# Adding transfers that no longer wait for transposing ones, in a convolution and feed-forward kernel

## The chip, the cores and the metric

One core of one Trainium2 chip. The metric is the device time of one execution in microseconds (us), as a median over runs.

## The reference, cut to what matters

Per head and token, seven weights are made by a softmax; they weigh the token and the six before it (a causal convolution whose weights depend on the position). A layer norm and a two-layer feed-forward block with a residual follow.

```python
batch, seq, d_model = (8, 4224, 192)      # 8 heads of 24 channels, 7 taps, 4 * 192 hidden channels
def _attn_ref(x, weight_gen):
    w = np.exp(weight_gen - np.max(weight_gen, axis=-1, keepdims=True))
    w = w / (np.sum(w, axis=-1, keepdims=True) + 1e-09)
    ...
    out = np.einsum('bshk,bskhg->bshg', w, x_unf)
def _moe_ref(x, g_ln, w_ch1, w_ch2):
    xn = (x - mu) / np.sqrt(var + 1e-06) * g_ln
    ch = np.maximum(xn @ w_ch1, 0.0) @ w_ch2
    return (x + ch).astype(np.float32)
```

## The kernel before, in words

**Tiling.** The 33,792 tokens lie on 128 partitions, 264 on each. They pass through in chunks of 4 tokens a partition (67 chunks; the first two have 2), the norm works on parts of 4 or 8, and the feed-forward block on 66 groups of 4, that is 512 tokens.

**Stages.** SP loads x and the softmax's input. The softmax (L466 to L499) runs on VectorE, GpSimd and ScalarE. For a chunk, VectorE multiplies x by the weights, two taps at a time, into buffers `pr` and, for one tap, into `y` (L544). The seven results are then summed. Adding transfers do part of it: GpSimd issues a DMA that adds one half of a `pr` buffer to its other half (`dma_add`, L550; two for each chunk from the fifth on, 126 in all). GpSimd itself adds four buffers to `y` (L547, 252 times); a `pr` buffer is free for VectorE's next product when GpSimd has read it. There are seven `pr` buffers. ScalarE takes sums and squares for the norm (L597, L602), normalises into `xh` (L657) and copies it to fp16, the upper part of `hl` (L677); GpSimd subtracts for the lower part (L690). Then a transposing transfer, issued by SP, turns `hl` into `xT` (L694, one for each group, 66 in all). There are two `hl` buffers and three `xT` buffers.

**Feed-forward block.** TensorE makes the hidden layer of a group in three units of 36 products each (L712) into two PSUM buffers `ph` in turn. ScalarE (relu, L727) and VectorE (the rest, L729) evict a unit; when VectorE's eviction ends, the buffer is free for the next unit but one. The output of an earlier group follows in two halves of 72 matmuls (L763) between the units; the second half waits for a nop on SP (L773) behind the first. VectorE adds the residual (L815), SP stores (L823).

**Order.** Every operation has a place in one list, written out by hand (`PLACE`, L32 to L226). `Plan.order` (L272) sorts by it, picks buffers, and so fixes the order on every engine and queue; engines take their instructions in that order and wait by semaphores. The same function keeps two kinds of transfer apart. An operation may have a kind: "add" for the adding transfers (L576), "turn" for the transposing ones (L694, through `sp`). `last` holds the latest operation of each of these two kinds, and `o.behind` is the latest one of the other kind (L287, L288). After all operations have been issued, L1016 and L1017 make an instruction wait until the transfer in `o.behind` has landed. So an adding transfer, issued by GpSimd, waits for the last transpose ahead of it in the list, and a transpose, issued by SP, for the last adding transfer. What stands behind a waiting instruction in the same engine's order waits too.

Of the kernel before, what the change touches and what calls it, by code (L numbers as in the profile page):

```python
# [238 lines left out]
class Plan:  # L239
# [32 lines left out]
    def order(self):  # L272
        out = sorted(self.ops, key=lambda o: o.place)
        tenant = {p: [None] * len(t) for p, t in self.pools.items()}
        done, last = set(), {"add": None, "turn": None}

        def freed(t):
            return -1 if t is None else max(x.place for x in t.ops)

        for o in out:  # L280
            assert o.deps <= done, "an operation is placed ahead of what it needs"
            for b in o.bufs:
                if b.slot is None:
                    b.slot = min(range(len(tenant[b.pool])), key=lambda i: freed(tenant[b.pool][i]))
                    assert freed(tenant[b.pool][b.slot]) < o.place, "no buffer is free"
                    tenant[b.pool][b.slot] = b
            if o.kind in last:  # L287
                o.behind, last[o.kind] = last["turn" if o.kind == "add" else "add"], o  # L288
            done.add(o)
        return out  # L290

# [756 lines left out]
```

## Time and profile before

| | |
|---|---|
| Time, median of 3 runs | 856.57 us (855.5 to 859.03) |
| Profiled execution: its time, its span | 856.96 us, 855.2 us |
| TensorE (PE) busy | 823.4 us, 96% |
| VectorE (DVE) busy | 763.0 us, 89% |
| GpSimd (POOL) busy | 728.7 us, 85% |
| ScalarE (ACT) busy | 646.1 us, 76% |
| Transposing transfers, adding transfers | 66, 126 |
| Mean granted TensorE clock | 0.992 |

All times inside the execution count from the start of the span. An instruction's row gives its start, its duration, its engine, line and operation, what it writes and reads, how many equal ones are merged, and in brackets how long the engine had been idle before it and what ended that. "DMA xT<-hl" is the landing of a transposing transfer, "DMA pr<-pr" that of an adding one. A duration of a matmul includes its passage through the pipeline, so matmuls overlap, and their pitch is shorter than their duration.

### The profile page before, as it was taken

The numbers are of one execution on the slowest core, as the hardware profiler recorded it, in microseconds if no ns is written. First come the engines' busy times: TensorE is split into PE (matmuls) and PEld (weight loads), VectorE is DVE, ScalarE is ACT, GpSimd is POOL, SyncE is SP. The second block draws the span as 40 slices with busy tenths as digits, with TensorE's granted clock in tenths as the row PEclk, the third lists the DMA queues.
The fourth block names the chain that finished last, engine by engine and source line by source line (L and its number), as shares of the span: only waits on it lengthen the run. The fifth ranks groups of instructions, "written<-read, shape, count | busy, mean of one in ns | idle before, by whom it ended". The sixth has DMA issues, their size and how long they took to land. (4 is left out here: it accounts for less than half of the span.)

```text
span 855.2 us, 37740 instructions
## 1 busy us (share of the span) xinstructions
PE 823.4 (96%) x16691; PEld 803.7 (94%) x16691; DVE 763.0 (89%) x863; ACT 646.1 (76%) x1797; POOL 728.7 (85%) x489
## 2 busy tenths in 40 slices
PE   4959999999999999999999999999999899999997
PEld 4548999999999999999999999999999899999997
DVE  7999999999999999999999999999999899673442
ACT  3888898787778888778869887878878678667521
POOL 7999999999899999999999889999986878964100
PEclk9979999999999999999999999999999999999999
DMA  9878878898878898788988799798876675845123
GB/s 219 192 176 171 166 153 186 162 199 192 188 169 198 192 190 162 181 164 189 203 187 203 163 184 197 165 168 198 190 152 151 159 137 134 158 80 108 37 74 94
DMA packets 146411, 140.91 MB, mean 165 GB/s; under 512 B 108487, under 2 KB 110415, under 8 KB 146247
## 3 DMA queue, kind: packets, MB, share of 16 engines
q1 hardware_dynamic: 127799, 88.95, 44.3%
q0 software_dynamic: 18144, 49.55, 31.3%
q8 instruction: 130, 2.13, 1.1%
q14 instruction: 34, 0.28, 0.1%
q10 hardware_dynamic: 304, 0.00, 0.0%
HBM read 36.43 MB, written 25.95 MB: 73 GB/s over the span
## 5 line engine op out<-in xcount | busy, mean ns | idle before, releaser
L547 POOL TENSOR_TENSOR y<-y,pr 128x768 f32<-128x768 f32 x252 | 514.2, 2206 | 15.4 <-DMA pr<-pr 6.1
L712 PE MATMUL ph<-xT,c_w 64*128 64x256 f16 x7128 | 417.0, 271 | 8.4 <-DVE hlo L729 8.0
L712 PEld LDWEIGHTS <-c_w 64*128 64x128 f16 x7128 | 383.8, 95 | 17.0 <-issue 11.1
L763 PE MATMUL po<-c_w2h,hh 64*128 64x192 f16 x3120 | 387.8, 243 | 0.8 <-SPq L773 0.4
L763 PE MATMUL po<-c_w2h,hlo 64*128 64x192 f16 x3120 | 387.8, 243 | 0.0
L763 PE MATMUL po<-c_w2l,hh 64*128 64x192 f16 x3120 | 387.7, 243 | 0.0
L544 DVE TENSOR_TENSOR pr<-x,wn 128x1536 f32<-128x1536 f32 (+1 forms) x193 | 332.1, 1738 | 5.5 <-POOL y L547 3.9
L763 PEld LDWEIGHTS <-hh 64*128 64x128 f16 x6240 | 307.2, 94 | 2.1 <-SPq L773 1.0
L729 DVE SCALAR_TENSOR_TENSOR hlo<-ph,hh 128x1024 f16<-128x1024 f32 x198 | 239.5, 1217 | 55.8 <-ACT hh L727 55.7
L727 ACT ACTIVATE hh<-ph 128x1024 f16<-128x1024 f32 x198 | 199.4, 1013 | 117.3 <-PE ph L712 114.8
L763 PEld LDWEIGHTS <-hlo 64*128 64x128 f16 x3120 | 175.3, 94 | 0.0
L690 POOL TENSOR_TENSOR hl<-xh,hl 128x768 f16<-128x768 f32 x66 | 132.8, 2031 | 33.3 <-ACT hl L677 33.2
L550 POOL DMA_DIRECT2D pr<-pr x126 | 130.1, 1233 | 27.4 <-DMA xT<-hl 14.4
L657 ACT ACTIVATE xh<-y,s 128x192 f32<-128x192 f32 x264 | 125.1, 535 | 22.1 <-DVE s L641 11.9
L602 ACT ACTIVATE junk<-y,s 128x192 f32<-128x192 f32 x264 | 116.1, 443 | 0.0
L597 ACT ACTIVATE junk<-y 128x192 f32<-128x192 f32 x264 | 92.2, 351 | 27.9 <-POOL y L547 27.5
L815 DVE SCALAR_TENSOR_TENSOR y<-po,c_fs,y 128x768 f32<-128x768 f32 (+1 forms) x66 | 65.7, 997 | 3.3 <-PE po L763 3.3
L544 DVE TENSOR_TENSOR y<-x,wn 128x768 f32<-128x768 f32 (+1 forms) x67 | 62.1, 933 | 0.2
L677 ACT ACTIVATE hl<-xh 128x768 f16<-128x768 f32 x66 | 55.0, 837 | 4.2 <-DMA xT<-hl 3.3
L602 ACT ACTIVATION_READ_ACCUMULATOR junk<-y,s 128x1 f32 x264 | 50.0, 189 | 0.0
L597 ACT ACTIVATION_READ_ACCUMULATOR junk<-y 128x1 f32 x264 | 49.8, 189 | 0.0
L469 POOL TENSOR_TENSOR e<-w,mx 128x672 f32<-128x672 f32 (+2 forms) x23 | 39.4, 1713 | 2.8 <-DVE mx L467 2.7
(75 smaller groups left out, 315.3 us busy)
## 6 DMA issues: line engine op xcount, KB each, us to landing
pr<-pr POOLq DMA_DIRECT2D x126, 384.0 KB, 6.2
x<-in_x_dram SPq DMA_DIRECT2D x65, 384.0 KB, 5.5
out_dram<-y SPq DMA_DIRECT2D x64, 384.0 KB, 4.4
w<-in_weight_gen_dram SPq DMA_DIRECT2D x21, 336.0 KB, 5.0
pr<-in_moe_w_ch_dram SPq DMA_DIRECT2D x2, 576.0 KB, 5.1
xT<-hl SPq DMA_TRANSPOSE x66, 3.6
hh<-in_moe_w_ch_dram SPq DMA_DIRECT2D x1, 768.0 KB, 10.1
out_dram<-y SPq DMA_DIRECT2D x4, 192.0 KB, 3.2
```

Of the source, the lines that this page charges most:

```text
L544: E.tensor_tensor(out=ov, in0=xv, in1=wv, op=ALU.mult)
L547: Q.tensor_tensor(out=flat(0), in0=flat(0), in1=flat(k), op=ALU.add)
L550: return Q.dma_start(flat(to), flat(k), accum_op=ALU.add, max_dma_last_dim=CHUNK * D * 4)
L597: A.activation(junk[t % 2], at(y)[:, j, :], AF.Identity, scale=-1.0 / D, accum_out=at(s4)[:, 3, t : t + 1])
L602: A.activation(junk[2 + t % 2], at(y)[:, j, :], AF.Square, bias=at(s4)[:, 3, t : t + 1], accum_out=at(s4)[:, 0, t : t + 1])
L657: A.activation(paired(xh, t), at(y)[:, i, :].rearrange("p (c q) -> p c q", q=P // 2), AF.Identity, bias=at(s4)[:, 3, g + t : g + t + 1], s ...
L690: lambda xh=xh, hl=hl: Q.tensor_tensor(out=halves(hl, True), in0=pairs(xh), in1=halves(hl, False), op=ALU.subtract),
L712: T_.matmul(ph[:, r, v * 2 * P : (v + 1) * 2 * P], W["w1"][rows, WB[r][c], w, f : f + P], xv[rows, a, c, :, :], start=(v == 0 and k == 0), ...
L727: lambda: A.activation(at(hh)[:, us, :], at(ph), AF.Relu), [ph], [(hh, u)])
L729: lambda: V.scalar_tensor_tensor(out=at(hlo)[:, us, :], in0=at(ph), scalar=0.0, in1=at(hh)[:, us, :], op0=ALU.max, op1=ALU.subtract),
L763: made.append(T_.matmul(at(po)[:, z, e * D : (e + 1) * D], token(b, 2 * z + e, j)[rows], W[w][rows, j, :], start=(ph == 0 and e == 0 and k ...
L815: V.scalar_tensor_tensor(out=ysl, in0=at(po)[:, zs[0] : zs[-1] + 1, : 2 * D], scalar=W["fs"][:, 0:1], in1=ysl, op0=ALU.mult, op1=ALU.add)
```

## The change

An adding transfer gets no `o.behind` any more, so L1017 makes no wait for it. A transposing transfer still gets the last adding one. Order, buffers and all other waits come from the same list as before.

```diff
             if o.kind in last:
-                o.behind, last[o.kind] = last["turn" if o.kind == "add" else "add"], o
+                o.behind, last[o.kind] = last["add"] if o.kind == "turn" else None, o
             done.add(o)
```

## Rows read from the trace of the kernel before

**Rows 1.** The page's part 1: engine, busy us (share of the span), instructions.
```profile
PE 823.4 (96%) x16691; PEld 803.7 (94%) x16691; DVE 763.0 (89%) x863; ACT 646.1 (76%) x1797; POOL 728.7 (85%) x489
```
**Rows 2.** Waits of PE: who waited for whom, us in total, times, longest.
```profile
PE ph L712 <- DVE hlo L729: 8.0, 9, 2.3
```
**Rows 3.** Timeline of PE around its two late gaps: start us, us, what.
```profile
668.53 0.26 PE L763 MATMUL po<-c_w2l,hh 64*128 64x192 f16 x2
668.61 0.26 PE L763 MATMUL po<-c_w2h,hlo 64*128 64x192 f16 x2
...
671.13 3.56 PE L712 MATMUL ph<-xT,c_w 64*128 64x256 f16 x36 [2.26 <-DVE hlo L729]
...
677.73 0.51 PE L712 MATMUL ph<-xT,c_w 64*128 64x256 f16 x6
...
748.66 0.26 PE L763 MATMUL po<-c_w2h,hlo 64*128 64x192 f16 x2
749.95 0.40 PE L712 MATMUL ph<-xT,c_w 64*128 64x256 f16 x4 [1.03 <-DVE hlo L729]
```
**Rows 4.** Stretches: length, busy us (instructions) of PE, PEld, DVE, ACT, POOL, clock, DMA share, GB/s.
```profile
671.10:672.00 0.90, 0.87 (x14) 0.84 (x15) 0.86 (x2) 0.67 (x1) 0.90 (x2) 0.81 0.98 321
672.00:673.00 1.00, 1.00 (x14) 0.85 (x11) 1.00 (x2) 0.17 (x1) 1.00 (x2) 0.50 1.09 215
```
**Rows 5.** The chain of work that ended last, in order of time: start us, us, what.
```profile
646.01 7.56 DMA pr<-pr
...
653.70 4.11 DMA xT<-hl
...
684.81 1.97 PE ph L712 x36
686.77 2.97 PE po L763 x72
```
**Rows 6.** Timeline of DVE, 600 to 673 us and at 748 us.
```profile
640.09 3.41 DVE L544 TENSOR_TENSOR pr<-x,wn 128x1536 f32<-128x1536 f32 x2
...
660.45 0.17 DVE L630 TENSOR_SCALAR wn<-s 128x8 f32<-128x8 f32 x1 [1.75 <-ACT junk L602]
660.53 1.22 DVE L729 SCALAR_TENSOR_TENSOR hlo<-ph,hh 128x1024 f16<-128x1024 f32 x1
...
668.19 1.75 DVE L544 TENSOR_TENSOR pr<-x,wn 128x1536 f32<-128x1536 f32 x1 [2.17 <-POOL y L547]
...
748.67 1.23 DVE L729 SCALAR_TENSOR_TENSOR hlo<-ph,hh 128x1024 f16<-128x1024 f32 x1 [3.99 <-ACT hh L727]
```
**Rows 7.** Timeline of ACT, the waits ahead of the two gaps.
```profile
657.83 0.84 ACT L677 ACTIVATE hl<-xh 128x768 f16<-128x768 f32 x1 [1.42 <-DMA xT<-hl]
...
745.36 0.36 ACT L597 ACTIVATE junk<-y 128x192 f32<-128x192 f32 x1 [3.29 <-POOL y L547]
```
**Rows 8.** Waits of POOL: who waited for whom, us in total, times, longest.
```profile
POOL pr L550 <- DMA xT<-hl: 14.4, 9, 4.9
```
**Rows 9.** Timeline of POOL: its long waits for a transpose, and the subtraction at 661.06.
```profile
504.51 2.66 POOL L550 DMA_DIRECT2D pr<-pr  x3 [2.45 <-DMA xT<-hl]
...
625.98 1.77 POOL L550 DMA_DIRECT2D pr<-pr  x2 [1.80 <-DMA xT<-hl]
...
643.10 1.77 POOL L550 DMA_DIRECT2D pr<-pr  x2 [1.53 <-DMA xT<-hl]
...
658.09 0.87 POOL L550 DMA_DIRECT2D pr<-pr  x1 [4.91 <-DMA xT<-hl]
...
661.06 2.25 POOL L690 TENSOR_TENSOR hl<-xh,hl 128x768 f16<-128x768 f32 x1
...
725.99 3.57 POOL L550 DMA_DIRECT2D pr<-pr  x4 [1.68 <-DMA xT<-hl]
```
**Rows 10.** Timeline of PE, the product that uses the transpose of 653.70.
```profile
661.80 4.11 PE L712 MATMUL ph<-xT,c_w 64*128 64x256 f16 x72
```
**Rows 11.** Issue to landing of all transfers of a line: L694 transposing, then L550 adding.
```profile
DMA to landing us min/median/max: 3.2/3.6/6.5
...
DMA to landing us min/median/max: 3.8/6.2/10.7
```

## The prediction

> **What bounds the kernel now.** I read the page first. TensorE is busy for 823.4 us of a span of 855.2 [rows 1], so only time in which TensorE stands still, or runs slowly, can be won. The table of waits narrows this: from the first product to the last, the products waited 8.0 us in nine pieces for VectorE's eviction, which frees the PSUM buffer that the next product writes [rows 2]. The timeline of TensorE places them. Four pieces lie before 70 us, while the pipeline fills, and three are small. Two large ones lie late [rows 3]. At 668.61 the last output matmul starts; its neighbours follow 0.08 us apart, so the next was due at 668.69, and it starts at 671.13: 2.44 us. At 748.66 the same: due 748.74, started 749.95: 1.21 us.
>
> The first of the two costs more than its gap. Behind it the granted clock falls to 0.81 and then to 0.50 [rows 4], half speed. So 36 products and 72 output matmuls, which elsewhere take 1.97 and 2.97 us (4.94 together; the chain of work has both [rows 5]), run from 671.13 to 677.73, 6.60 us [rows 3]: 1.66 us lost to the clock. Behind the gap of 1.21 us no such stretch follows. The two places cost 2.44 + 1.66 + 1.21 = 5.31 us.
>
> Next question: who made VectorE late? In its timeline [rows 6] the late eviction stands behind a product that started at 668.19, after an idle 2.17 us that a GpSimd sum ended (sums free the buffers that products write). Before that VectorE had idled 1.75 us for ScalarE. The eviction of 748.67 waited for ScalarE, and ScalarE's timeline shows why: it stood idle 3.29 us until GpSimd's sum at 745.36 [rows 7]. Both roots are GpSimd being late. GpSimd's own waits name the cause: 14.4 us in nine pieces were spent ahead of an adding transfer until a transposing one had landed [rows 8]. These are just the waits that the change takes away.
>
> **The change, part by part.** It adds no instruction and moves none; 126 adding transfers lose one wait each. Most lose nothing real: by the time GpSimd reached them, the transpose had landed. Only the nine pieces are time, and GpSimd's timeline shows the large ones [rows 9]: 2.45 us at 504.51, 1.80 at 625.98, 1.53 at 643.10, 4.91 at 658.09 and 1.68 at 725.99 (some half a microsecond of two or three of them is the issue itself).
>
> The wait at 504.51 is worth nothing: neither large gap of TensorE lies within 160 us behind it, so products already waiting in buffers hide it. If that cover is gone it is 2.45 us at most.
>
> The first gap. Ahead of it GpSimd loses 1.80 + 1.53 + 4.91 = 8.24 us. Not all of this comes back, because the transposes still wait for adding transfers. Follow the chain of work [rows 5]: the adding transfer of 646.01 takes 7.56 us, and right behind its landing the transpose is sent at 653.70, taking 4.11 us. That transfer was held by the first two waits (3.3 us), but it also needs VectorE's products that end at 640.09 + 3.41 = 643.50 [rows 6]; it can be sent some 2.4 us sooner. So can the transpose, and ScalarE's copy, which idled 1.42 us until that transpose landed [rows 7], and the subtraction that GpSimd starts at 661.06 behind the copy [rows 9]; with the queue of GpSimd empty earlier, that one gains between 2.4 and 4.9 us. The product on VectorE needs 2.17 us. Its idle 2.17 us goes, most of the earlier 1.75 us with it: VectorE is up to 2.17 + 1.75 = 3.9 us earlier there. TensorE then has no gap, keeps its clock, and is 2.44 + 1.66 = 4.10 us earlier. VectorE is 0.2 us short of that, and I give 0.2 us back.
>
> The second gap. GpSimd must be 4.1 + 1.2 = 5.3 us earlier at 745.36 than now. It brings some 3.9 us from before and gains the 1.68 us at 725.99: 5.6 us. This is close, but enough. None of the nine pieces lies behind 750 us: from there TensorE runs through to its end, so what is won reaches the end of the run.
>
> What is late next: VectorE, whose evictions end just ahead of TensorE's need in this stretch. One ends at 660.53 + 1.22 = 661.75 [rows 6], and the product that needs its buffer starts at 661.80 [rows 10]. The issue queue of SP has no more to do; the nops by which the output matmuls change banks stand behind transposes in it as before.
>
> The operation that this trace doesn't have is an adding transfer sent while a transpose is in flight: now neither starts before the other has landed. I bound it from the two groups of landings [rows 11]. A transpose takes 3.2 us at best and up to 6.5 us, and it does meet plain loads and stores; an adding transfer takes 3.8 to 10.7 us. The lower end is no slowing: 3.2 us. The upper is one after the other: 3.2 + 10.7 = 13.9 us. I take 6.5 us at most, since plain transfers on the same queues are nearest to it. The transpose of 653.70 is needed by the product of 661.80 [rows 5, 10], 8.1 us later, so 6.5 us costs nothing, and it would itself be sent 2.4 us sooner.
>
> **The sum.** The profiled execution took 856.96 us (span 855.2 us and 1.8 us around it), 0.4 us over the median of 856.57. 5.31 - 0.2 = 5.1 us less gives 851.9 us for that execution and 851.5 us against the median. A measurement of this kernel can tell about 0.5%, 4.3 us, from no change: faster means below 852.3 us.
>
> **The rivals.**
> *Only the first gap goes.* The four adding transfers of 725.99 are sent sooner but land no sooner, since they now run beside a transpose; GpSimd's sums then wait for the landing instead. The 1.21 us stay: 856.57 - 4.10 = 852.5 us. For it speaks how close the second account was; against it, that these transfers have 3.8 to 10.7 us to land in [rows 11] and the late sum comes 19 us behind them. The Trainium skill, on the page "DMA: Bandwidth & Descriptors", section "Issuing engines are not separate DMA queues", says that transfers started by different engines run on the same 16 DMA engines and interleave, so starting them side by side saves little beyond the issue; by this rule the time is that of this rival, 852.5 us. The trace agrees so far as transposes stretch from 3.2 to 6.5 us.
>
> *VectorE becomes the bound.* GpSimd runs ahead, but the evictions keep TensorE back right after 671 us, and a gap of some 2 us opens there in small pieces. Half of the 2.44 us stays in this way, the clock's 1.66 us are won, and the second gap stays: 1.22 + 1.66 = 2.9 us less, 853.7 us. For it: the margin of 0.05 us just shown. Against it: VectorE's own idle time ahead of the gap was caused by GpSimd.
>
> *The change removes nothing.* ScalarE's copy and the subtraction behind it still wait for a transpose through the buffers, and take the place of the wait: 856.6 us. Against it: the copy's own waits were 1.42 us where GpSimd's was 4.91.
>
> *Slower.* Adding transfers and a transpose in flight hinder each other much more than plain ones. The place is the transpose of 653.70; it decides from 8.1 us on. At 13.9 us it lands at 667.6, TensorE stands for 5.8 us at 661.80, pays the slow clock again (1.7 us), and the old gaps stay because adding transfers land late too: 856.57 + 5.8 + 1.7 = 864.1 us. Nothing here shows that pair, which is why it keeps a chance.
>
> *More.* The small pieces of TensorE's 8.0 us go by the shift as well, with the 0.2 us that I gave back and a wait or two of the output matmuls: about 1.3 us, an estimate, 850.2 us.
>
> **How the numbers follow.** Forecast 0.45, only the first gap 0.17, VectorE 0.14, nothing 0.08, more 0.08, slower 0.08. Of the forecast, about 0.38 lies below 852.3 us; of the first rival 0.07, and all of "more": 0.53 faster. Slower has its rival's 0.08. The other 0.39 is within 0.5%. The range goes from 849.9 us (the better case and the spread of the runs) to 856.9 us (no change); it leaves out the slower rival and the outer parts of two others.
>
> **What would show it.** Right: no wait of an adding transfer for a transpose in GpSimd's table; no gap of TensorE over 1 us after 70 us; a granted clock of 1.00 from 600 to 700 us; TensorE's last product about 5 us earlier. Wrong: the 0.50 stretch still there, or a new wait of GpSimd's sums for the adding transfers, or transposes that take over 8 us. If the products wait for xT itself, the slower rival holds; if they wait for the eviction at other places, VectorE's.

## The result and the profile after

The changed kernel takes 849.37 us, the median of 4 runs (849.22 to 849.53); the kernel before took 857.56 us beside it (4 runs, 855.50 to 859.03). The ratio is 0.9906 [0.9883, 0.9930]. A second set, run later, gave 849.37 us again (5 runs, 849.22 to 849.62) and a ratio of 0.9923 [0.9909, 0.9937]. So the change wins 0.8 to 0.9%, some 7 us. That is the direction forecast, but 2.1 us more of it than the 851.5 us forecast, and 0.5 us below the lower end of the range, 849.9 us.

Part 1 of the page of the changed kernel (span 847.6 us, 855.2 before), beside [rows 1]:

```profile
PE 819.1 (97%) x16691; PEld 802.6 (95%) x16691; DVE 762.4 (90%) x863; ACT 646.1 (76%) x1797; POOL 727.7 (86%) x489
```

The engines run the same number of instructions. TensorE is busy for 4.3 us less: 1.66 us of it is the half-speed stretch, which is gone, and 1.1 us lies within the first 70 us (47.77 us busy before, 46.63 after), which the change hardly touches: the product that starts at 136.88 us starts 0.10 us later (table below). The span is 7.6 us shorter. So busy time alone does not tell where the gain lies; the stretches and the starts below do.

Waits of PE in the changed kernel (who waited for whom: us in total, times, longest), beside [rows 2]:

```profile
PE ph L712 <- DVE hlo L729: 5.1, 6, 2.2
```

Waits of POOL in the changed kernel, the longest kinds:

```profile
POOL hl L690 <- ACT hl L677: 38.2, 12, 19.2
POOL pr L550 <- DVE pr L544: 13.6, 7, 4.1
...
POOL y L547 <- DMA pr<-pr: 1.6, 3, 1.0
```

The 14.4 us of [rows 8] have no row any more. Two of the kinds that are left were shorter in the kernel before:

```profile
POOL hl L690 <- ACT hl L677: 33.2, 8, 19.1
POOL pr L550 <- DVE pr L544: 7.2, 4, 4.1
```

So part of the waiting came back in another form: GpSimd, now ahead, waits 5.0 us more for ScalarE's copies and 6.4 us more for the products that it adds. What went is the waiting for GpSimd: VectorE's products stood 3.9 us for GpSimd's sums before and stand 0.6 us now. The sums themselves wait 1.6 us for adding transfers, 6.1 us before.

Stretches of the changed kernel: length, busy us (instructions) of PE, PEld, DVE, ACT, POOL, then the clock, DMA share, GB/s:

```profile
70.00:600.00 530.00, 529.14 (x11252) 524.62 (x11250) 523.97 (x577) 435.42 (x1229) 513.40 (x343) 1.00 0.86 182
600.00:700.00 100.00, 100.00 (x2127) 99.95 (x2123) 96.21 (x104) 79.45 (x230) 86.88 (x59) 1.00 0.84 168
700.00:760.00 60.00, 60.00 (x1286) 60.00 (x1283) 46.75 (x48) 44.80 (x125) 47.97 (x33) 1.00 0.61 119
```

The same stretches of the kernel before:

```profile
70.00:600.00 530.00, 528.17 (x11208) 521.73 (x11205) 522.13 (x575) 434.10 (x1228) 511.78 (x342) 1.00 0.85 181
600.00:700.00 100.00, 97.62 (x2041) 96.71 (x2037) 92.56 (x101) 74.91 (x213) 82.66 (x55) 0.98 0.72 155
700.00:760.00 60.00, 58.97 (x1256) 58.76 (x1253) 46.05 (x46) 46.95 (x135) 51.25 (x35) 1.00 0.66 133
```

From 600 to 760 us TensorE now stands still for nothing at all, at a granted clock of 1.00: both late gaps of [rows 3] and the half-speed stretch of [rows 4] are gone. But the first line has changed too: 530.00 - 528.17 = 1.83 us of idle time ahead of 600 us became 0.86 us. The forecast had no term for that.

Where the time came from is read best from the products' own starts. The table takes the first product of some feed-forward groups and sets its start against the profiled execution of the kernel before (us; negative is earlier). The last column but one is the kernel before itself, profiled once more.

| Start in the kernel before | changed kernel | kernel before again | only late adds freed (e1) |
|---|---|---|---|
| 136.88 | +0.10 | +0.17 | +0.37 |
| 149.11 | -0.16 | +0.68 | +0.21 |
| 541.55 | -0.80 | +0.10 | -0.36 |
| 554.44 | -1.43 | -0.47 | -0.91 |
| 625.99 | -1.97 | -0.60 | -1.11 |
| 689.56 | -6.32 | -2.63 | -5.50 |
| 761.81 | -7.56 | -1.93 | -6.74 |

The changed kernel wins 1.97 us up to 626 us and 7.56 - 1.97 = 5.59 us behind it; against the second profile of the kernel before it is 1.37 and 4.26 us. Nothing is won or lost behind 762 us.

GpSimd's timeline at places of [rows 9], in the changed kernel:

```profile
501.08 2.65 POOL L550 DMA_DIRECT2D pr<-pr  x3
...
648.37 0.87 POOL L550 DMA_DIRECT2D pr<-pr  x1
```

The adding transfers of 504.51 are issued at 501.08 and the one of 658.09 at 648.37, neither behind any idle time.

### The profile page after: what moved, and what is told of

It is laid out like the page before. It is cut to its first block, busy times and chain, and to the rows that moved or that the text cites. A ratio compares the mean times of both kernels' runs of the same rounds, so it can differ in the third digit from the quotient of the medians.

```text
span 847.6 us, 37758 instructions
## 1 busy us (share of the span) xinstructions
PE 819.1 (97%) x16691; PEld 802.6 (95%) x16691; DVE 762.4 (90%) x863; ACT 646.1 (76%) x1797; POOL 727.7 (86%) x489
## 5 line engine op out<-in xcount | busy, mean ns | idle before, releaser
L547 POOL TENSOR_TENSOR y<-y,pr 128x768 f32<-128x768 f32 x252 | 505.7, 2159 | 13.9 <-DVE y L544 5.9
L690 POOL TENSOR_TENSOR hl<-xh,hl 128x768 f16<-128x768 f32 x66 | 126.7, 1938 | 40.2 <-ACT hl L677 38.2
L550 POOL DMA_DIRECT2D pr<-pr x126 | 127.7, 1196 | 15.2 <-DVE pr L544 13.6
```

The lines of the kernel that those rows point to most:

```text
L547: Q.tensor_tensor(out=flat(0), in0=flat(0), in1=flat(k), op=ALU.add)
L550: return Q.dma_start(flat(to), flat(k), accum_op=ALU.add, max_dma_last_dim=CHUNK * D * 4)
L690: lambda xh=xh, hl=hl: Q.tensor_tensor(out=halves(hl, True), in0=pairs(xh), in1=halves(hl, False), op=ALU.subtract),
```

## The experiments

The kernel before scatters from 852.5 to 860.7 us over the 73 runs that stand beside these kernels, so each ratio is against the runs of its own set. Each edit changes what an operation waits for through `o.behind` and nothing else. Where one code line is added, the profile's line numbers are one higher (L551 for L550). "Place" is the operation's place in the hand-written list.

### Which part of the program holds the gain

**e1_late** frees only the adding transfers from the one at 625.98 on.

```diff
-                o.behind, last[o.kind] = last["turn" if o.kind == "add" else "add"], o
+                free = o.kind == "add" and o.place >= 2195
+                o.behind, last[o.kind] = None if free else last["turn" if o.kind == "add" else "add"], o
```

> Only the last 30 of the 126 adding transfers are freed of their wait, from the one sent at 625.98 us in the trace of before; the 106 ahead of it keep theirs... counted by place, those from place 2195 on. Theory (two late gaps of TensorE hang on these waits alone): both gaps and the slow clock go, 5.3 us less than before (4.8 to 5.8), and the small gaps before 600 us stay. Rival (the gain is spread: many small waits each cost a little): about 2 us less, and one of the large gaps still stands.

**e2_early** frees only those ahead of it (`o.place < 2195`).

> The opposite part: only the adding transfers ahead of place 2195 are freed, the late ones keep their wait. Theory: the two late gaps stay; what goes are small gaps before 600 us, 0.5 to 2.3 us less. Rival (an early lead of GpSimd is carried along): GpSimd comes to 625 us earlier and the large gaps shrink, 4 us less or more.

(By the issues in the trace the split is 24 late and 102 early adding transfers; where these texts count otherwise, that is a slip.)

Measured: e1 851.31 us (7 runs, 850.41 to 854.26), ratio 0.9949 [0.9926, 0.9972]; e2 854.02 us (11 runs, 852.27 to 855.23), ratio 0.9973 [0.9959, 0.9986]. Both intervals lie below 1. Taken on 856.5 us (the runs of the kernel before have medians of 855.8 to 857.8 us in the five sets), that is 4.4 us for the late part and 2.3 us for the early one, together 6.7; the whole change wins 6.6 in the set where its ratio is 0.9923. Stretches of e1, columns as above:

```profile
600.00:700.00 100.00, 100.00 (x2123) 99.81 (x2120) 96.47 (x105) 78.71 (x230) 87.85 (x60) 1.00 0.84 168
700.00:760.00 60.00, 60.00 (x1286) 60.00 (x1283) 46.77 (x47) 44.76 (x122) 47.10 (x32) 1.00 0.60 117
```

And of e2:

```profile
70.00:600.00 530.00, 529.52 (x11256) 524.82 (x11254) 524.11 (x577) 435.43 (x1229) 513.27 (x343) 1.00 0.86 182
600.00:700.00 100.00, 98.34 (x2076) 97.58 (x2072) 93.75 (x102) 78.55 (x229) 84.38 (x59) 1.00 0.76 160
700.00:760.00 60.00, 59.15 (x1260) 58.93 (x1257) 45.85 (x47) 42.44 (x117) 48.01 (x31) 1.00 0.65 126
```

With the late adding transfers free, TensorE has no idle time from 600 to 760 us. With only the early ones free it keeps 1.66 + 0.85 us of it there, and loses only 0.48 us ahead of 600 us. The late part was forecast at 5.1 us and measures 4.4; the early part was forecast at nothing and measures 2.3. The intervals are wide, 2.4 to 6.3 us for the late part and 1.2 to 3.5 us for the early one. Set against the steady 849.37 us of the changed kernel, e1, which keeps the early waits, loses 1.9 us, and e2, which keeps the late ones, 4.7 us.

**e4_again** is the kernel before once more, unchanged, for a second profile.

> The kernel before, unchanged, a second time. If the small gaps of TensorE (140.7, 255.9, 334.3, 543.4, 550.8 us) stand at the same places with the same size, they belong to the schedule and the change must have taken some of them away; if they wander between executions, up to 2 us of the gain is the spread of the kernel before. The two late gaps should stand again, within 0.5 us of 2.44 and 1.21 us, with the stretch of half clock behind the first.

Measured: 855.95 us (11 runs, 854.32 to 857.48), ratio 0.9999 [0.9986, 1.0011]. Its stretches:

```profile
600.00:700.00 100.00, 98.16 (x2082) 97.44 (x2079) 93.07 (x101) 76.79 (x219) 83.71 (x58) 1.00 0.74 157
700.00:760.00 60.00, 58.45 (x1245) 58.04 (x1241) 45.98 (x47) 44.44 (x128) 50.43 (x33) 1.00 0.67 130
```

The clock stays at 1.00, and the idle time lies in five pieces of 0.6 to 1.1 us (667.73, 675.30, 681.33, 700.65, 746.95) instead of one of 2.44 and one of 1.21. By the products' starts this execution loses 5.59 - (1.93 - 0.60) = 4.26 us against the changed kernel behind 626 us. The half-speed stretch stands in no other profiled execution of this document: in all the others the granted clock is 1.00 from 70 to 845 us, even in e12, where TensorE stands idle for 2.43 us at a time. So the two late gaps, and above all the 1.66 us of slow clock, are the shape of one execution; the second loses about 4.3 us there by other gaps, near the 4.4 us that e1 wins. The early gaps wander too: that at 141 us is larger here (0.73 us idle, 0.22 in the first profile), and that at 551 us is absent.

### Whether one wait makes the first late gap

**e3_one** takes away one wait only, the 4.91 us at 658.09.

```diff
+                free = o.kind == "add" and o.place == 2292
+                o.behind, last[o.kind] = None if free else last["turn" if o.kind == "add" else "add"], o
```

> One single adding transfer is freed, the one that waited 4.91 us at 658.09. Theory (this wait is the root of the first gap): the first gap falls under 0.5 us, TensorE keeps full clock, the second gap stays: 4.1 us less (3.5 to 4.5). Rival (the transpose of 653.70, held by the two waits ahead, keeps ScalarE's copy and GpSimd's subtraction late): the gap is only halved, 1 to 2.5 us less.

Measured: 854.57 us (11 runs, 853.54 to 858.54), ratio 0.9989 [0.9973, 1.0005]. My theory of about 4 us fell; what is left, 1.0 us, is not clear of noise, and the interval (0.4 us over to 2.3 us under) also holds most of the rival's 1 to 2.5 us. The table of POOL's waits shows where it went:

```profile
POOL pr L551 <- DMA xT<-hl: 8.1, 6, 4.4
```

The longest wait is again 4.4 us. It stands at the next adding transfer, which waited for the same transpose to land: freeing one of two neighbours only hands the wait on.

**e8_four_back** goes the other way: the changed kernel with four of the long waits put back (625.98, 643.10, 658.09, 725.99).

```diff
-                o.behind, last[o.kind] = last["add"] if o.kind == "turn" else None, o
+                free = o.kind == "add" and o.place not in (2195, 2238, 2292, 2502)
+                o.behind, last[o.kind] = None if free else last["turn" if o.kind == "add" else "add"], o
```

> The changed kernel with four of the 126 waits put back: the adding transfers that stood waiting at 625.98, 643.10, 658.09 and 725.99 us. Theory (the late gain hangs on these four): the late gaps come back, 4 us or more over the changed kernel, about 2 to 3 us under before. Rival (the lead that GpSimd gains earlier covers them, or other waits matter): under 1.5 us over the changed kernel.

Measured: 851.92 us (5 runs, 851.12 to 852.89), ratio 0.9952 [0.9938, 0.9965]; that is 2.55 us over the changed kernel in the same set. It lies between the theory and the rival. TensorE's timeline has three small gaps:

```profile
667.00 2.14 PE L713 MATMUL ph<-xT,c_w 64*128 64x256 f16 x36 [0.40 <-DVE hlo L730]
674.43 2.14 PE L713 MATMUL ph<-xT,c_w 64*128 64x256 f16 x36 [0.36 <-DVE hlo L730]
679.97 2.14 PE L713 MATMUL ph<-xT,c_w 64*128 64x256 f16 x36 [0.43 <-DVE hlo L730]
```

Each is 0.55 to 0.6 us by the pitch: the last output matmul ahead of the first starts at 666.34, the next was due 0.08 us later and starts at 667.00. A fourth, of 1.1 us, ends at 745.13. Together 2.8 us, against 2.55 measured. Four waits do not restore the whole loss, and the gap of 2.44 us does not come back in one piece.

**e9_back_2412, e10_back_2502, e11_back_2292** each put one wait back into the changed kernel: that of 697.64, of 725.99 and of 658.09 (`o.place != 2412` and so on in the line of e8).

> The changed kernel with one wait put back: that of the adding transfer which the trace of before sends at 697.64 us, after 3.28 us that the profile puts down to issue. Theory (this wait, which the prediction passed over, is a third late place; a gap of about 1 us at 700 us stood in every trace that kept it but the first): a gap near 694 us, 0.5 to 1.3 us over the changed kernel. Rival (the wait is hidden once GpSimd has its lead): within 0.3 us of the changed kernel.

> The changed kernel with one wait put back: that of the first of the four adding transfers of 725.99 us. Theory (this one wait is the whole of the second gap): a gap of 1.0 to 1.2 us near 742 us and 1.1 us over the changed kernel, nothing else. Rival (the lead from the other freed waits covers it): under 0.4 us.

> The changed kernel with one wait put back: that of the adding transfer of 658.09 us. Theory (this wait alone costs what the first gap is, because the transpose that it waits for is itself held by adding transfers until then): GpSimd waits 3 to 5 us there, the gaps from 666 to 680 us come back, 1.3 to 2 us over the changed kernel. Rival (GpSimd's lead at that place is enough): the wait is under 2 us and the time within 0.4 us of the changed kernel.

Measured: e9 849.61 us (5 runs, 849.36 to 851.69), ratio 0.9930 [0.9908, 0.9952]; e10 850.30 us (850.11 to 850.64), 0.9933 [0.9910, 0.9956]; e11 849.43 us (849.20 to 849.78), 0.9923 [0.9902, 0.9943]. POOL's waits of e9, then of e10, then of e11:

```profile
POOL pr L551 <- issue: 3.3, 1, 3.3
```

```profile
POOL pr L551 <- DVE hlo L730: 2.1, 1, 2.1
```

```profile
POOL pr L551 <- DMA xT<-hl: 2.1, 1, 2.1
```

Each wait that was put back is there, though only e11's table names the transpose: the others are put down to "issue" and to an eviction that had long ended, so this kind of wait has to be found by the idle time ahead of L551. Against the changed kernel's 849.37 us, which comes from two other sets of runs, a wait of 3.3 us and one of 2.1 us cost 0.2 and 0.1 us, within the scatter (e9, of whose five runs one took 851.69 us, and e11), and one of 2.1 us costs 0.9 us (e10). TensorE's timeline of e10 shows it:

```profile
743.60 2.61 PE L713 MATMUL ph<-xT,c_w 64*128 64x256 f16 x44 [0.85 <-DVE hlo L730]
```

One wait, that of 725.99, is therefore enough to make the second late gap, as forecast. The first is nobody's alone: with all other waits away, that of 658.09 shrinks to 2.1 us and is hidden. I take it that waits there add up until GpSimd's lead is spent; no run shows that by itself.

### What the early waits cost, and by which way

**e12_turns_early** leaves every wait of an adding transfer in place and frees the early transposing ones instead, to see whether SP's half of the pairing makes the early loss.

```diff
+                free = o.kind == "turn" and o.place < 2195
+                o.behind, last[o.kind] = None if free else last["turn" if o.kind == "add" else "add"], o
```

> The kernel before, but the transposing transfers ahead of place 2195 don't wait for adding ones; all adding transfers keep their waits. This takes the waits for landings out of SP's queue before 625 us. Theory (the small early gaps come from SP: a transpose waits there for an adding transfer to land, and the nop that TensorE's second half needs stands behind it): no gap at 141 and 551 us, and 0.5 to 1.5 us under before; the late gaps stay. Rival (the early gaps come from GpSimd's own waits): they stay, and so does the time.

Measured: 857.11 us (11 runs, 853.12 to 862.84), ratio 1.0013 [0.9988, 1.0037]. The theory's win is not seen; the interval leaves room for 1.0 us of it at most. The profiled execution took 861.53 us, 4.4 us over the median, so its rows show places and not typical sizes. The small gap at 141 us does go. But SP's freed transposes now fly beside adding transfers (up to 10.4 us from issue to landing, 6.5 before), GpSimd waits for them longer, and TensorE stands still elsewhere, for 1.74 us ahead of 393.64 us and for 2.43 us ahead of 556.03. POOL's waits, then TensorE's timeline, of e12:

```profile
POOL pr L551 <- DMA xT<-hl: 16.3, 9, 4.5
```

```profile
556.03 0.26 PE L764 MATMUL po<-c_w2h,hh 64*128 64x192 f16 x2 [2.43 <-SPq L774]
```

The last row names SP's nop (L774 here), for which the second half of an output waits. It is the half that starts at 551.46 us in the kernel before. So that gap does not need SP's waits for adding transfers: here SP has none of them ahead of 625 us, and the gap is the larger for it.

**e13_back_first, e14_back_1773, e15_back_middle** are the changed kernel with early waits put back: those of the 48 adding transfers up to about 300 us (`place < 1100`), that of 504.51 alone, and those from 300 to 620 us (`1100 <= place < 2195`).

> The changed kernel with the waits of the first 48 adding transfers put back (those ahead of 300 us). Theory (part of the early gain comes from the place at 141 us, where TensorE's second half waits for a nop behind SP's wait for an adding transfer): 0.4 to 1 us over the changed kernel, with a gap at 141 us in at least some executions, so that the runs spread by more than 0.5 us. Rival (nothing early matters): within 0.2 us of the changed kernel, and as steady.

> The changed kernel with one wait put back, that of the adding transfer which stood 2.45 us at 504.51 us, the one that the prediction costed at nothing. Theory (GpSimd is then 2 to 3 us later up to 551 us, its subtraction sends the transpose late, and the nop behind the transpose's issue holds TensorE): 0.3 to 1 us over the changed kernel, with a gap at 551 us. Rival (as the prediction said, nothing): within 0.2 us.

> The changed kernel with the waits of the adding transfers between about 300 and 620 us put back. Theory (the places from 540 to 650 us carry the larger half of the early gain): 1 to 2 us over the changed kernel, spread over 1 us or more. Rival (the early gain is all at 141 us): within 0.3 us.

Measured: e13 850.92 us (6 runs, 850.16 to 853.94), ratio 0.9925 [0.9897, 0.9953]; e14 849.66 us (849.59 to 850.39), 0.9909 [0.9886, 0.9932]; e15 851.22 us (850.61 to 851.54), 0.9924 [0.9901, 0.9947]. Against the nine runs of the changed kernel in two other sets, none over 849.62 us, that is 1.5, 0.3 and 1.9 us more. So the wait of 504.51, the largest of the early ones in the trace, is worth little (it is back in e14 with 2.2 us, and the gap expected at 551 us is not there). The rest hangs on smaller ones, which were not taken apart further. The two halves do not add up: together they cost 3.4 us, while e1, which keeps both, loses 1.9. In the profiled execution of e13, 2.5 us over its median, 1.05 us of the 3.61 us that it loses to the changed kernel lie ahead of 626 us; most of the rest is one late gap, shown under "What stays open".

Two places show how an early wait reaches TensorE, and they are not alike. At 141 us an output begins. TensorE's timeline in the kernel before run again, in e13 and in the changed kernel:

```profile
141.89 0.26 PE L763 MATMUL po<-c_w2h,hh 64*128 64x192 f16 x2 [0.73 <-DVE y L815]
```

```profile
141.92 0.26 PE L764 MATMUL po<-c_w2h,hh 64*128 64x192 f16 x2 [0.77 <-DVE y L816]
```

```profile
141.04 0.26 PE L763 MATMUL po<-c_w2h,hh 64*128 64x192 f16 x2
```

The expectations of e12 and e13 took this for a second half behind SP's nop. It is a first half, and its nop comes behind it (145.06 us in the kernel before run again). The rows name VectorE's residual, which reads an earlier output from PSUM, and VectorE is late there. A sum of the softmax on VectorE, in the same three kernels:

```profile
133.45 0.85 DVE L476 TENSOR_REDUCE sm<-e 128x96 f32<-128x672 f32 x1 [0.92 <-ACT e L472]
```

```profile
133.49 0.85 DVE L477 TENSOR_REDUCE sm<-e 128x96 f32<-128x672 f32 x1 [0.96 <-ACT e L473]
```

```profile
132.61 0.85 DVE L476 TENSOR_REDUCE sm<-e 128x96 f32<-128x672 f32 x1
```

VectorE idles for an exponential of ScalarE, and this for a subtraction of GpSimd, which stands behind the adding transfers in GpSimd's order. The chain in the kernel before run again:

```profile
128.57 2.66 POOL L550 DMA_DIRECT2D pr<-pr  x3 [0.34 <-DMA xT<-hl]
130.25 2.37 POOL L469 TENSOR_TENSOR e<-w,mx 128x672 f32<-128x672 f32 x1
```

```profile
132.66 0.77 ACT L472 ACTIVATE e<-e 128x672 f32<-128x672 f32 x1 [2.11 <-POOL e L469]
```

```profile
140.82 1.02 DVE L815 SCALAR_TENSOR_TENSOR y<-po,c_fs,y 128x768 f32<-128x768 f32 x1
```

In the changed kernel the adding transfers leave at 127.76 us, the subtraction starts at 129.44 and the exponential at 131.81, each 0.8 us earlier. From the softmax's sum to the residual VectorE has no pause, so the delay arrives whole: the residual ends at 141.84 us, and TensorE starts at 141.89. All 17 profiled executions fit this. In the five in which the softmax's sum idles, for 0.24 to 0.96 us, TensorE idles there for 0.2 us less; in the others, where it idles 0.18 us at most, TensorE does not stand. So the loss at 141 us goes through ScalarE and VectorE, as that of the late gaps does, and not through SP.

At 551 us the way is SP's queue: a second half stands there for the nop. GpSimd's subtraction and SP's queue, in the kernel before:

```profile
548.27 1.64 POOL L690 TENSOR_TENSOR hl<-xh,hl 128x768 f16<-128x768 f32 x1
```

```profile
549.94 1.42 SPq L694 DMA_TRANSPOSE xT<-hl  x1
```

In the changed kernel:

```profile
544.83 1.65 POOL L690 TENSOR_TENSOR hl<-xh,hl 128x768 f16<-128x768 f32 x1
```

```profile
546.51 1.46 SPq L694 DMA_TRANSPOSE xT<-hl  x1
```

And TensorE in e15, with SP's queue there:

```profile
550.92 0.26 PE L764 MATMUL po<-c_w2h,hh 64*128 64x192 f16 x2 [0.60 <-SPq L774]
```

```profile
549.39 1.42 SPq L695 DMA_TRANSPOSE xT<-hl  x1
```

The transpose is issued as soon as the subtraction ends, and the issue alone holds SP's queue for 1.42 us. The nop behind it releases TensorE's second half: 549.39 + 1.42 = 550.81, and TensorE starts at 550.92, late by 0.6 us. In the changed kernel the subtraction is 3.4 us earlier, and the nop is out of the way at 548.0. The kernel before shows the same wait for L773 at 551.46 in its first profile, where the table above has the step from -0.80 to -1.43, and not in its second: this loss too comes and goes. The same half waits 1.63 us in e6 (below) and 2.43 us in e12.

### Whether the other half of the pairing matters

**e5_neither** takes both kinds of wait away, **e6_reverse** frees the transposes and keeps the adding transfers waiting; **e7_after_again** is the changed kernel unchanged, beside them.

```diff
-                o.behind, last[o.kind] = last["turn" if o.kind == "add" else "add"], o
+                o.behind, last[o.kind] = None, o                                        # e5
+                o.behind, last[o.kind] = last["turn"] if o.kind == "add" else None, o   # e6
```

> Both waits are taken away: transposing transfers no longer wait for adding ones either. Theory (TensorE is held only through GpSimd's waits, and those are gone already in the changed kernel): as the changed kernel within 1 us, some 7 us under before, with transposes landing earlier and nobody using it. Rival (transposes and adding transfers hinder each other once they overlap freely): transposes beside adding transfers take over 8 us, GpSimd's sums wait more for landings, and the time is over the changed kernel's by 2 us or more.

> The other half alone: transposing transfers don't wait for adding ones, adding ones wait for transposing ones as in the kernel before. Theory (the gaps come from the two waits taking turns, so that breaking either side is enough): transposes are sent as soon as GpSimd's subtraction ends, have landed before GpSimd reaches the next adding transfer, GpSimd waits under 5 us instead of 14.4, and 4 to 7 us are won. Rival (only the wait on GpSimd's own queue matters): its waits stay near 14 us and under 2 us are won.

> The changed kernel, a second time, beside the others of this call. Expected: its time is steady to within 0.5 us and 0.8 to 1.0% under before (848.5 to 850), with no gap of TensorE over 0.6 us after 70 us. If instead it spreads over 5 us like the kernel before, the steadiness was chance.

Measured: e5 849.20 us (5 runs, 849.09 to 851.05), ratio 0.9926 [0.9910, 0.9942]; e6 854.71 us (11 runs, 853.34 to 859.63), 0.9986 [0.9965, 1.0006]; e7 849.37 us, given above. Freeing the transposes as well adds nothing to the change; freeing them alone wins 1.2 us by the medians, and the interval includes none. Waits of POOL, then of PE, in e6:

```profile
POOL pr L550 <- DMA xT<-hl: 10.2, 3, 5.1
```

```profile
PE po L763 <- SPq L773: 1.6, 1, 1.6
```

GpSimd still waits, up to 5.1 us at a time, and so TensorE does. All of the gain that is clear of noise is on GpSimd's side. Issue to landing of the transposing transfers, in the changed kernel, in e5 and in e6, where 3.2/3.6/6.5 is the row of before [rows 11]:

```profile
DMA to landing us min/median/max: 3.2/3.9/6.5
```

```profile
DMA to landing us min/median/max: 3.2/4.7/7.6
```

```profile
DMA to landing us min/median/max: 3.2/4.5/9.3
```

In the changed kernel eight of the 60 transposes whose landing the trace has flew beside an adding transfer; they took 3.56 to 5.72 us. No version here beats the changed kernel by more than its runs scatter.

## Why the prediction was wrong in its size

**What held.** The root was GpSimd waiting for transposes. Those waits went, and GpSimd's longer waits for its inputs leave TensorE without idle time from 600 to 760 us. Both late gaps closed, the clock stayed at 1.00 from 600 to 700 us, and there is no gap over 0.5 us behind 70 us. Those were the signs named for the forecast. The late part came to 5.59 us on the trace that the sum was made from, against 5.31 - 0.2 = 5.1. The 0.2 us that I gave back for VectorE were not due: of the two waits of VectorE counted there (2.17 and 1.75 us), 0.2 us is left.

**The step that failed** is the first paragraph of the part-by-part account: "Most lose nothing real", with "The wait at 504.51 is worth nothing" and the later "the nops by which the output matmuls change banks stand behind transposes in it as before". The sum has no term ahead of 600 us. It measured 2.3 us when the early waits alone were taken away (e2), 1.9 us when they alone were left (e1), and 1.5 and 1.9 us when either half of them was put back (e13, e15). The sentence on 504.51 by itself was nearly right (0.3 us, e14), and it was the wrong question. I looked for large gaps of TensorE near large waits of GpSimd, and found none. The early loss is small delays, of which two were followed: at 141 us a late adding transfer makes GpSimd's subtraction, ScalarE's exponential and so VectorE late (0.2 to 0.8 us of idle TensorE); at 551 us a late subtraction sends a transpose late, and the nop for TensorE stands behind it in SP's order (0.45 to 0.6 us). How the rest of the 2.3 us reaches TensorE stays open. By the medians, the miss of 2.1 us is this term (2.3), less the 0.7 us by which the late part was too large (below), plus some 0.5 us of scatter in the few runs of the kernel before; each of these is known to about 1 us or worse.

**A second size, perhaps too large.** The late part of 5.1 us was built on one execution. The second profile of the kernel before loses 4.3 us there, with other gaps and no slow clock, and freeing the late part alone wins 4.4 us (e1). By these the term was 0.7 us too large for a typical run, though e1's interval still holds 5.1. That it came near is in part luck: 1.66 us of it was a slow clock that no other execution shows, and other gaps took its place. The nine pieces were not all, either: the 3.28 us at 697.64 us, which the table puts down to "issue", was such a wait too (e9), worth 0.2 us by itself. The first gap was put down to three waits of 8.24 us; e3, e8 and e11 show that it follows none of them singly.

**The rivals.** *Only the first gap goes* (852.5 us) fell: 725.99 is the cause of the second gap (e10), and sums wait only 1.6 us for adding transfers. The Trainium skill, on the page "DMA: Bandwidth & Descriptors", section "Issuing engines are not separate DMA queues", says that starting transfers side by side saves little but the issue. What was saved here was not transfer time, which hardly changed (the adding transfers' median is 6.0 us after and 6.2 before, the transposes' 3.9 and 3.6), but time in which an engine with other work stood behind a wait; on this the rule says nothing, and the 852.5 us that it gave were not measured. *VectorE becomes the bound* fell: the 5.1 us that products still wait for it lie ahead of 70 us, but for pieces under half a microsecond. *The change removes nothing* fell with the time: the subtraction does wait 5.0 us more for ScalarE's copies, but the copies wait for no transpose any more. *Slower* fell for the changed kernel: it decided from 8.1 us on for the transpose needed at 661.80. In the changed kernel that one flew 3.56 us, and was needed 9.3 us after it had landed. But its mechanism is there: beside adding transfers, transposes took up to 9.3 us in e6 and 10.4 us in e12, so that "6.5 us at most" holds in the changed kernel but not in every order, and in e13 it was this very transpose (next paragraph). *More* came nearest in time (850.2 us), and its "wait or two of the output matmuls" names the right operations at 141 and 551 us. But it took its 1.3 us mainly from the small pieces of [rows 2], most of which are still there.

**What stays open.** In the profiled execution of e13 a gap of 1.94 us opened at 662.89, though all late adding transfers were free. SP's queue, then GpSimd and ScalarE, ahead of it:

```profile
649.55 1.42 SPq L695 DMA_TRANSPOSE xT<-hl  x1
```

```profile
649.56 0.88 POOL L551 DMA_DIRECT2D pr<-pr  x1
...
651.94 1.19 POOL L551 DMA_DIRECT2D pr<-pr  x1
```

```profile
658.91 0.84 ACT L678 ACTIVATE hl<-xh 128x768 f16<-128x768 f32 x1 [3.19 <-DMA xT<-hl]
```

The transpose is the one of 653.70 in the kernel before. With two adding transfers issued 0.01 and 2.39 us behind it, it landed after 9.3 us; ScalarE's copy waited 3.19 us for it, VectorE 3.52 us for ScalarE, and TensorE for VectorE's eviction. This is what *Slower* feared, by another way than the product that it named. The same transpose took 3.5 and 3.6 us in the two profiles of the changed kernel, 6.97 in e10 and 6.7 in e14, without such a gap. Two of e13's six runs took over 853 us; whether the other is the same was not seen. The nine runs of the changed kernel, within 0.40 us of one another, show no sign of it. Nor is it settled why the transpose sent near 123 us took 4.8 and 5.4 us in two executions of the kernel before and 3.2 in the changed one.

## What to carry to other kernels

Cost a removed wait not only at the engine that waited, but along every engine and queue that waits for what this engine does next. At 141 us the delay went through two engines that have no part in the transfer; at 551 us a late transpose delayed an unrelated release behind it in the same queue. Follow the chain from the row that waits back to its start, and do not take two rows that move together for one that holds the other. Take the loss that a change may remove from two executions of the kernel before, not from the gaps of one. Where several waits delay the same engine in turn, their effect is not a sum: one taken away hands its delay to the next, and one put back is hidden.

## What the runs showed that was not expected

**The scatter went with the waits.** The kernel before ranges over 8.2 us in 73 runs (852.47 to 860.66); the changed kernel over 0.40 us in nine (849.22 to 849.62). Kernels that keep a few of the waits lie between (e11 0.6 us, e15 0.9, e9 2.3, e1 and e13 3.8, in five to seven runs), and e6 and e12, which keep all of GpSimd's, range over 6.3 and 9.7 us in eleven. A range grows with the number of runs, and e5, which has no waits of either kind, has 2.0 us in five. With GpSimd waiting, a transpose that is late by chance seems to pass its delay on, and with GpSimd free it seems to be absorbed, mostly. That link was not measured by itself.

**The issue of a transpose is long on its queue.** It holds SP for 1.4 us at the median in the kernel before (1.42 at 549.94; 2.7 at most), where a store holds it for 0.60 (144.30 in the changed kernel): what stands behind a transpose in that queue is late by this even when nothing is waited for.
